# A fixed reserve behind tiles written by GpSimd and by transfers, in the rule that chooses the next instruction of TensorE

## The chip, the cores and the metric

The kernel runs on 1 core of one Trainium2 chip. The metric is the device time of one execution in microseconds; shown is the median of several runs. TensorE (PE) multiplies, VectorE (DVE), ScalarE (ACT) and GpSimd (POOL) do the elementwise work, and SyncE (SP) issues every transfer (DMA). Each engine takes its instructions strictly in the order in which the program lists them for it, and an instruction that needs another engine's result waits on a semaphore, with everything that stands behind it.

## The reference

Four sublayers on a sequence of 2048 rows of 512 numbers: attention with a compressive memory (32 heads of 16, four segments of 512 rows, each causal in itself, and a memory that is carried from segment to segment), a Fourier mixing by two DFT matrices, and both once more.

```python
x = A_x
x = x + _A_ref(_layernorm(x, axis=-1), A_wq, A_wk, A_wv, A_wo, A_beta)
x = x + _B_ref(_layernorm(x, axis=-1), B_dft_seq_re, B_dft_seq_im, B_dft_hid_re, B_dft_hid_im)
x = x + _A_ref(_layernorm(x, axis=-1), A_wq, A_wk, A_wv, A_wo, A_beta)
x = x + _B_ref(_layernorm(x, axis=-1), B_dft_seq_re, B_dft_seq_im, B_dft_hid_re, B_dft_hid_im)

def _A_ref(x, wq, wk, wv, wo, beta):      # q, k, v = x @ w, by heads and segments
    ...
    for s in range(N):
        logits = jnp.einsum("bhqd,bhkd->bhqk", qs, ks) * scale + mask
        p = _softmax(logits, axis=-1)
        a_dot = jnp.einsum("bhqk,bhkd->bhqd", p, vs)
        a_mem = num / den                 # phi(q) @ M  /  phi(q) @ z
        o = g * a_mem + (1.0 - g) * a_dot
        M = M + jnp.einsum("bhld,bhle->bhde", pk, vs)
    ...

def _B_ref(x, dft_seq_re, dft_seq_im, dft_hid_re, dft_hid_im):
    a = jnp.einsum("bsd,ed->bse", x, dft_hid_re)
    b = jnp.einsum("bsd,ed->bse", x, dft_hid_im)
    return jnp.einsum("ts,bse->bte", dft_seq_re, a) - jnp.einsum("ts,bse->bte", dft_seq_im, b)
```

## The kernel before

The work is cut into 32 groups, `i` from 0 to 31: two layers, four segments, four sets of eight heads. Sixteen generators (`streams`) each walk through one kind of work and, as they go, spawn short ones (`tasks`):

- `s_p` projects Q and K of a group, `s_v` projects V. Both multiply the normalized, transposed rows `xt` (tile `g`) with a weight tile. From the second segment on, the weight tile is loaded again from DRAM by `weights.get`, when a slot of its kind (`wt`, `wv`) is free.
- `s_x` computes the scores once for their row maxima: `t_max` on DVE writes them into `mx`, TensorE transposes `mx` by `identf`, and four small transfers write the result into spare rows of `qst`. `s_st` computes the scores a second time, transposed; `t_sel` takes their exponential on ACT into a tile of kind `pt` and masks that tile on GpSimd with `affine_select`; `s_av` multiplies it with `vt`, the values.
- `s_mem` reads and updates the memory `macc`; `s_m` and `t_merge` divide by the denominators through a round trip over DRAM (`den`, `rec`); `s_o` applies `wo`.
- `s_ab` applies the hidden DFT (`wd`), `s_f` the sequence DFT, whose factors `cc` are prepared in `s_c` and kept in DRAM for the second layer. `s_f` and `s_ab` supply the bulk of the wide 128x512 products, and these can stand beside the attention of another segment.

In PSUM all tiles come from one pool of eight banks (named `b`), in SBUF most come from one pool of fifty slots (named `w`); a tile's name carries slot and a running number.

Nothing of the order is written out by hand. While the program is built, the class `Plan` keeps a clock for each engine (`free`), and for each tile the time of its last write (`wr`), its last read (`rd`) and the engine that wrote it last (`by`; `V`, `G`, `A`, `T`, `Y` for DVE, GpSimd, ACT, TensorE, and SP's transfers). Every emitted instruction advances these by a price for its engine, kind and size (`op`). Before an instruction is emitted, a generator yields what it needs (`need`): the engine, the tiles read, the slots wanted. The loop at the end of `body` asks `pl.ready` of all waiting generators for the time at which their need is met, takes the larger of that and the engine's clock, applies a few rules for TensorE (below), and lets the earliest go on; at equal times the first in the list does. So these times decide only which instruction is emitted next. On the chip the semaphores alone hold an instruction back.

TensorE has three modes: `m` for products over the full array, `h` for the scores, which use half of its rows (two at a time), `v` for `s_av`, which uses a quarter of its columns (four at a time). `turn` makes a change of mode dearer in the planner by `SWITCH`, and two blocks in the loop put score work and `s_av` behind other work that is ready.

The price of a transfer in `op` is an issue of 440 ns, 650 ns, its bytes at 360 bytes per ns, and 950 ns behind a load, where the call gives no other estimate: 2768 ns for a weight tile of 256 KB.

Of the kernel before, what the change touches and what calls it, by code (L numbers as in the profile page):

```python
# [31 lines left out]
SLACK = 0  # L32
HOLD, SWITCH = 700.0, 95.0
TWICE, EARLY, BESIDE = 1000.0, 0.0, 1000.0
BATCH = 4
NR = 2


class Plan:
# [80 lines left out]
            ar, b = self.slot[t.tensor.name]  # L120
            self.count[ar["held"].pop(b)] -= 1

    def ready(self, reads, tags):
        r = self.slots_free(tags)
        if r is None:
            return None
        for t in reads:
            n = self.key(t)
            if n in self.fresh:
                return None  # L130
            r = max(r, self.wr.get(n, 0.0))
        return r

    def op(self, eng, name, args, kw):
# [110 lines left out]
def body(ctx: ExitStack, tc: tile.TileContext, x, wq, wk, wv, wo, beta, wd, cs, out):  # L245
    nc = tc.nc
    pl = Plan()
    V, G, A, T, Y = (Eng(e, k, pl) for e, k in zip(
        (nc.vector, nc.gpsimd, nc.scalar, nc.tensor, nc.sync), "VGATY"))
# [59 lines left out]
    def rg(tag, bufs, dt, shape=(128, 512)):  # L309
        return work.tile(list(shape), dt, name=tag, bufs=bufs)  # L310

    def need(eng, *reads, tag=(), mode="m"):
        return eng, reads, (tag,) if isinstance(tag, str) else tag, mode
# [352 lines left out]
    def weights(kind, which):  # L666
        order = [(n, i % NG) for i in range(NG, NGRP) for n in which]
        ready = []

        def get(j, n):  # L670
            if j < NG * len(which):
                yield gate(("W", n, j // len(which)))
                return wnow[n, j // len(which)]
            j -= NG * len(which)
            while len(ready) <= j or len(ready) < len(order) and pl.slots_free((kind,)) is not None:
                n, g = order[len(ready)]
                w = sb(kind, F16, (128, 2, KT, 128))
                Y.dma_start(w, wqkv[g][n])
                ready.append(w)
            return ready[j]  # L680
        return get
# [260 lines left out]
    def width(j):  # L942
        return len(chunks[j][1]) // 2
# [19 lines left out]
    def s_c():  # L963
        k = u = 0
        while u < nunit:
            n = width(units[u][0])
            cam, csc, cgm = (rg(t, 3, F32, (128, BATCH)) for t in ("cam", "csc", "cgm"))
            for i in range(k, k + BATCH):
                yield lambda: len(raws) > i
                yield need("V", raws[i])  # L970
                V.tensor_reduce(cam[:, i - k:i - k + 1], raws[i], axis=AX.X, op=OP.max, apply_absolute_value=True)
            m = BATCH // n
            yield need("T", cam, tag="dft")
# [11 lines left out]
            V.tensor_scalar(fyu[:, u:u + m], gv, f_y, None, op0=OP.mult)  # L985
            for i in range(k, k + BATCH):
                raw, sc = raws[i], csc[:, (i - k) // n:(i - k) // n + 1]
# [11 lines left out]
                done.add(("cd", i))  # L999
            k += BATCH  # L1000
            u += m
# [73 lines left out]
    def settle(s):  # L1075
        while callable(s[0]) and s[0]():
            s[0] = next(s[1], None)
        return s[0] is not None and not callable(s[0])

    while streams or tasks:  # L1080
        best = None
        moved = True
        while moved:
            moved = False
            for s in tasks + streams:
                if callable(s[0]) and s[0]():
                    settle(s)
                    moved = True
        tasks[:] = [s for s in tasks if s[0] is not None]
        streams[:] = [s for s in streams if s[0] is not None]  # L1090
        ready, raw = [], {}
        for s in tasks + streams:
            w = s[0]
            if not callable(w):
                r = pl.ready(w[1], w[2])
                if r is not None:
                    free = pl.turn(w[3]) if w[0] == "T" else min(pl.free[e] for e in w[0])
                    ready.append((max(r, free), s))
                    raw[id(s)] = r
        if pl.mode == "m":  # L1100
            other = min((r for r, s in ready if s[0][0] == "T" and s[0][3] == "m"), default=1e18)
            for j, (r, s) in enumerate(ready):
                if s[0][0] == "T" and s[0][3] == "v" and r >= other:
                    ready[j] = max(r, raw[id(s)] + BESIDE), s
        if pl.mode != "h":
            other = min((r for r, s in ready if s[0][0] == "T" and s[0][3] != "h"), default=1e18)
            for j, (r, s) in enumerate(ready):
                w = s[0]
                if w[2][:2] == ("ss", "ss") and r + EARLY >= other:
                    both = pl.ready(w[1], w[2] + ("ss", "ss"))  # L1110
                    late = raw[id(s)] + TWICE
                    ready[j] = max(r, late if both is None else min(both, late)), s
        if ready:
            first = min(r for r, _ in ready)
            best = next(q for q in ready if q[0] <= first + SLACK)
        if best is None:
            assert not streams and not tasks, "stuck"
            break
        best[1][0] = next(best[1][1], None)
# [45 lines left out]
```

## Time and profile before

| | us |
|---|---|
| median of 3 runs (1844.94 to 1851.16) | 1846.79 |
| the profiled execution's own time | 1845.85 |
| its span, first to last instruction | 1844.1 |
| DVE busy in it | 1086.3 (59%) |
| ACT busy in it | 897.4 (49%) |
| POOL busy in it | 722.6 (39%) |

TensorE's rows stand in the prediction. In all views a name such as `w` stands for every tile of its pool, and every instruction has the line 238, because a helper of the planner issues it; so groups are told apart by names and shapes: `b<-w,g` is the projection of V, `b<-g,w` that of Q or K, `b<-kst,qst` the scores of `s_x` and `b<-qst,kst` those of `s_st`, `b<-w,vt` the work of `s_av`, `b<-w,macc` and `b<-vt,w` reading and updating the memory, `b<-identf,mx` the transposes of the maxima. `w<-w` in a row of a DMA is a transfer between DRAM and a tile of the pool `w`; with TensorE's waits before `b<-w,g` and `b<-g,w` it is a weight tile.

### The profile page before, as it was taken

What the parts mean: (1) busy time and instruction counts of PE and PEld (TensorE: products, weight loads), DVE (VectorE), ACT (ScalarE), POOL (GpSimd) and SP (SyncE); (2) the same over time, 40 slices, a digit from 0 to 9 for tenths busy, and PEclk for the clock granted to TensorE, in tenths of its full rate; (3) what the DMA queues carried; (4) which work ended last, traced back from release to release, by engine and by line L of the source; (5) the groups of instructions that cost most, each with busy time, mean ns of one, the idle gap of its engine ahead of it and who ended that gap; (6) DMA issues with size and microseconds to landing.
All of it is one profiled execution on the core that took longest, in us unless ns stands there. A gap on an engine that the chain in (4) does not pass through costs nothing. (4 is left out here: it accounts for less than half of the span.)

```text
span 1844.1 us, 32657 instructions
## 1 busy us (share of the span) xinstructions
PE 1706.5 (93%) x11045; PEld 744.4 (40%) x11045; DVE 1086.3 (59%) x3406; ACT 897.4 (49%) x1563; POOL 722.6 (39%) x1156
## 2 busy tenths in 40 slices
PE   3878799999999999999899979999999999999999
PEld 2333344443444444344444333433444444434444
DVE  7686774757485786555566655465547565634311
ACT  2546657666647565644447555455444544261000
POOL 3234545546445463553434433433433334052000
PEclk8888999999999999999999988999999999999999
DMA  7345534665466453355774552545345443323233
GB/s 188 103 130 135 146 84 142 183 170 155 122 151 197 127 142 97 110 150 166 225 199 151 168 119 48 142 115 120 106 106 145 120 118 91 90 74 98 92 120 115
DMA packets 240984, 242.44 MB, mean 131 GB/s; under 512 B 129776, under 2 KB 152304, under 8 KB 240816
## 3 DMA queue, kind: packets, MB, share of 16 engines
q1 hardware_dynamic: 240816, 240.35, 47.2%
q8 instruction: 87, 1.43, 0.3%
q14 instruction: 81, 0.66, 0.1%
HBM read 152.96 MB, written 63.70 MB: 117 GB/s over the span
## 5 line engine op out<-in xcount | busy, mean ns | idle before, releaser
L238 PE MATMUL b<-w,w 128*128 128x512 f16 x3072 | 712.3, 380 | 2.6 <-POOL w L238 2.0
L238 PEld LDWEIGHTS <-w 128*128 128x128 f16 x4992 | 462.8, 99 | 623.1 <-issue 130.1
L238 POOL TENSOR_TENSOR w<-w,w 128x512 f16<-128x512 f32 (+1 forms) x314 | 379.4, 1212 | 436.7 <-ACT w L238 271.3
L238 ACT ACTIVATE w<-b,fac 128x512 f32<-128x512 f32 (+1 forms) x728 | 419.4, 655 | 160.9 <-PE b L238 151.7
L238 DVE CUSTOM_DVE_ANT_0 junk<-b,cmask 128x128 bf16<-128x128 f32 (+3 forms) x1024 | 438.7, 486 | 94.8 <-PE b L238 94.0
L238 POOL TENSOR_SCALAR_AFFINE_SELECT w<-w 128x128 f32<-128x128 f32 (+2 forms) x704 | 242.2, 357 | 312.3 <-ACT w L238 306.1
L238 DVE SCALAR_TENSOR_TENSOR y<-b,fyu,y 128x512 f32<-128x512 f32 x200 | 149.4, 747 | 209.0 <-PE b L238 208.4
L238 ACT ACTIVATE w<-b 128x512 f32<-128x512 f32 (+1 forms) x240 | 137.6, 600 | 229.2 <-PE b L238 221.4
L238 ACT ACTIVATE w<-w,csc 128x512 f16<-128x512 f32 (+1 forms) x256 | 181.6, 721 | 57.3 <-DVE csc L238 49.6
L238 PE MATMUL b<-g,w 128*128 128x512 f16 x768 | 194.6, 395 | 13.4 <-issue 9.8
L238 PE MATMUL b<-w,vt 128*32 128x512 f32 (+3 forms) x2048 | 190.0, 451 | 13.2 <-POOL w L238 12.7
L238 PE MATMUL b<-wd,w 128*128 128x512 f16 x768 | 178.1, 380 | 0.0
L238 ACT ACTIVATE w<-w 128x512 f16<-128x512 f32 (+1 forms) x144 | 90.9, 634 | 169.6 <-DVE w L238 135.7
L238 DVE SCALAR_TENSOR_TENSOR w<-b,w 128x512 f16<-128x512 f32 x128 | 87.8, 687 | 134.5 <-ACT w L238 132.1
L238 PE MATMUL b<-kst,qst 62*128 62x128 f16 (+3 forms) x1024 | 127.5, 312 | 11.6 <-ACT w L238 3.5
L238 PE MATMUL b<-qst,kst 64*128 64x512 f16 (+3 forms) x1024 | 120.9, 307 | 15.9 <-ACT w L238 5.4
L238 PE MATMUL b<-w,g 128*128 128x128 f16 x1536 | 102.0, 227 | 19.9 <-DMA w<-w 10.1
L238 PEld LDWEIGHTS <-g 128*128 128x128 f16 x1536 | 93.4, 102 | 35.6 <-issue 17.7
L238 PEld LDWEIGHTS b<-w,vt 128*32 128x32 f32 x2048 | 58.3, 110 | 110.6 <-issue 49.6
L238 PEld LDWEIGHTS <-kst 64*128 64x128 f16 x1024 | 38.1, 94 | 134.3 <-issue 125.8
L238 PE MATMUL b<-wo,w 128*128 128x512 f16 x384 | 91.2, 384 | 0.2 <-DVE w L238 0.2
L238 DVE DVE_READ_ACCUMULATOR2_ANT mx<- 128x1 f32 x1024 | 84.5, 83 | 0.0
(102 smaller groups left out, 889.4 us busy)
## 6 DMA issues: line engine op xcount, KB each, us to landing
w<-in_cs_dram SPq DMA_DIRECT2D x128, 256.0 KB
cc<-w SPq DMA_DIRECT2D x128, 256.0 KB
w<-cc SPq DMA_DIRECT2D x128, 256.0 KB
w<-w SPq DMA_DIRECT2D x96, 256.0 KB
d<-w SPq DMA_DIRECT2D x128, 128.0 KB
w<-rec SPq DMA_DIRECT2D x56, 256.0 KB
w<-in_x_dram SPq DMA_DIRECT2D x32, 256.0 KB
qst<-d SPq DMA_DIRECT2D x64, 128.0 KB
```

The costliest lines, as they stand in the source:

```text
L238: r = f(*args, **kw)
```

## The change

A table of four numbers is added. `ready` now knows the engine that asks, and where TensorE asks, each tile that it would read counts as written later than the planner's time for it: by 500 ns where GpSimd wrote it last, by 1000 ns where a transfer did, by nothing where DVE or ACT did. Other engines ask as before. The times kept in `wr` and in the clocks are not changed, so an instruction that is chosen in spite of the reserve is priced as before.

```diff
+RESERVE = dict(G=500.0, Y=1000.0, V=0.0, A=0.0)
...
-    def ready(self, reads, tags):
+    def ready(self, reads, tags, eng):
...
-            r = max(r, self.wr.get(n, 0.0))
+            r = max(r, self.wr.get(n, 0.0) + (RESERVE.get(self.by.get(n), 0.0) if eng == "T" else 0.0))
...
-                r = pl.ready(w[1], w[2])
+                r = pl.ready(w[1], w[2], w[0])
...
-                    both = pl.ready(w[1], w[2] + ("ss", "ss"))
+                    both = pl.ready(w[1], w[2] + ("ss", "ss"), w[0])
```

The set of products is the same (18016 rows on PE in both programs); their order differs from the first rows on. A running number in a name counts up over all engines as the program is written, so the difference of two numbers tells how much was written between them.

The first place is on PE, the projection of V for the sixteenth group. In the row `b0_9359<-w11_9311,g1_6862` the weight tile `w11_9311` is loaded from DRAM; its load is written where the number 9311 stands. Before:

```order
L238 MATMUL b0_9316<-kst0_102,qst0_104 128x512
L238 MATMUL b7_9320<-kst0_102,qst0_104 128x512
L238 MATMUL b6_9290<-w8_7784,w22_8962 128x512
L238 MATMUL b6_9290<-w17_7825,w22_8962 128x512
L238 MATMUL b2_9344<-wd_141,w27_8460 128x512
L238 MATMUL b0_9359<-w11_9311,g1_6862 128x128
```

and now, where the tile is `w15_9368`:

```order
L239 MATMUL b1_9387<-identf_108,mx_8889 32x128
L239 MATMUL b7_9390<-wd_141,w46_8442 128x512
L239 MATMUL b3_9422<-wd_141,w31_8501 128x512
L239 MATMUL b5_9429<-cam_9396,ones_121 128x4
L239 MATMUL b0_9442<-kst1_103,qst1_105 128x128
L239 MATMUL b4_9457<-kst1_103,qst1_105 128x256
L239 MATMUL b1_9479<-w15_9368,g1_6774 128x128
```

A row stands for all that read the same two tiles. Between the load and the projection stood nine wide products of the DFT (two rows of three on `w22`, one of three on `w27`) and two pairs of scores; now 24 wide ones (twelve on `w46`, twelve on `w31`) and twelve narrow scores stand there, so the distance of the numbers went from 48 to 111.

The second place is on PE too, one of the products of `s_av` in the twentieth group. It reads `pt` tiles, which ACT wrote from the score banks `b4_13856` and `b0_13872` (before) and GpSimd then masked. Before:

```order
L238 MATMUL b1_13692<-w3_13708,vt1_107 32x384
L238 MATMUL b5_13769<-g1_13199,w24_13534 128x512
L238 MATMUL b4_13856<-qst1_105,kst1_103 128x256
L238 MATMUL b0_13872<-qst1_105,kst1_103 128x256
L238 MATMUL b7_13889<-qst1_105,kst1_103 128x128
L238 MATMUL b1_13692<-w48_13862,vt1_107 32x256 x2
```

and now, where the scores are in `b4_13815` and `b6_13826`:

```order
L239 MATMUL b4_13815<-qst1_105,kst1_103 128x256
L239 MATMUL b6_13826<-qst1_105,kst1_103 128x256
L239 MATMUL b2_13751<-g1_13251,w13_13494 128x512
L239 MATMUL b7_13851<-qst1_105,kst1_103 128x128
L239 MATMUL b0_13863<-kst0_102,qst0_104 128x256
L239 MATMUL b5_13874<-g1_13251,w8_13547 128x512
L239 MATMUL b7_13903<-kst0_102,qst0_104 128x384
L239 MATMUL b3_13628<-w34_13821,vt1_107 32x256 x2
```

Before, only eight narrow score products (on `b7_13889` and its partner) stood between the second pair of score banks and the product that reads the masked tile; now 18 wide products of Q and K (nine on `w13`, nine on `w8`) stand there as well.

## The prediction

> **What bounds the kernel now.** I read the page first, for the busy shares, then the waits of PE, the same waits split by stage, and single waits in the order of time.
>
> ```profile
> span 1844.1 us, 32657 instructions
> ...
> PE 1706.5 (93%) x11045; PEld 744.4 (40%) x11045; DVE 1086.3 (59%) x3406; ACT 897.4 (49%) x1563; POOL 722.6 (39%) x1156
> ```
>
> PE is busy for 93% of the span; no other engine reaches 60%. So TensorE is the bound, and the change can only gain where PE stands idle (1844.1 - 1706.5 = 137.6 us) or runs at a lower clock. The idle time before PE's instructions, by what ended it:
>
> ```profile
> PE b L238 <- POOL w L238: 26.9, 26, 5.1
> PE b L238 <- DVE mx L238: 26.3, 22, 3.9
> PE b L238 <- ACT w L238: 17.2, 23, 3.5
> PE b L238 <- DVE amax L238: 16.6, 3, 11.5
> PE b L238 <- DMA w<-w: 11.6, 10, 3.3
> ```
>
> The columns are us in total, times, longest. GpSimd ends 26.9 us; weight tiles that come by transfer end 11.6 us, and with the smaller rows of the split below transfers end 19 us. So some 46 us are all that the two reserves aim at. The rest, DVE and ACT above all, has a reserve of zero. Where these waits stand matters, because a reserve helps only where PE has other work to take:
>
> ```profile
> 0.00:260.00 260.00, 189.47 (x1354) 83.62 (x1355) 196.48 (x684) 129.26 (x230) 97.37 (x171) 0.88 0.52 138
> 260.00:1040.00 780.00, 750.41 (x4853) 333.00 (x4852) 495.97 (x1516) 458.66 (x778) 375.39 (x544) 0.99 0.54 153
> 1040.00:1120.00 80.00, 64.43 (x455) 25.68 (x454) 47.94 (x178) 45.36 (x83) 33.84 (x66) 0.83 0.51 128
> 1120.00:1660.00 540.00, 521.82 (x3552) 220.46 (x3551) 298.24 (x956) 255.05 (x461) 201.78 (x362) 1.00 0.41 107
> 1660.00:1845.00 185.00, 180.41 (x836) 81.61 (x834) 47.70 (x74) 9.09 (x15) 14.26 (x14) 1.00 0.33 106
> ```
>
> The columns are stretch, length, busy time of PE, PEld, DVE, ACT, POOL, then the granted clock, the DMA share and GB/s. In the head (to 260 us) PE is idle for 70.5 us: only the first groups exist there, so other work is scarce. From 260 to 1660 us it is busy 95% of the time, and the reserve can choose among many products; the gain has to come from there. In the last 185 us the sequence DFT runs alone.
>
> ```profile
> PE b L238 <- POOL w L238: 14.3, 12, 5.1
> ...
> PE b L238 <- DMA qst<-mhl: 3.3, 2, 2.5
> ```
>
> ```profile
> PE b L238 <- POOL w L238: 12.6, 14, 2.4
> PE b L238 <- DMA w<-w: 11.6, 10, 3.3
> ...
> PE b L238 <- DMA kst<-d: 2.2, 4, 0.8
> PE b L238 <- DMA g<-w: 1.3, 1, 1.3
> ...
> PE b L238 <- DMA qst<-mhl: 0.6, 1, 0.6
> ```
>
> The first two rows are the waits of the head, the others those after 260 us: 12.6 us behind GpSimd in 14 waits, and 11.6 + 2.2 + 1.3 + 0.6 = 15.7 us behind transfers in 16. With the head's 3.3 us the transfers make 19.0.
>
> **The change, part by part.** Nothing is added to or taken from the work of TensorE; only its order changes, and with it that of what follows on every engine. So the price is a sum of waits. The first three terms can't lie below nothing in themselves, since a reserve only adds work ahead of the reader; what the work taken first costs is the fourth.
>
> *Transfers after 260 us.* Two single rows show what the planner has wrong.
>
> ```profile
> 704.42 0.82 PE L238 MATMUL b<-w,g 128*128 128x128 f16 x6 [3.28 <-DMA w<-w]
> ...
> 1406.11 3.94 DMA w<-w
> ...
> 1530.22 2.75 DMA w<-w
> ...
> 170.65 2.75 PE L238 MATMUL b<-g,w 128*128 128x512 f16 x12
> ```
>
> The first is the longest wait for a weight tile, the next two are steps of the chain that ended last: from issue to landing such a load took 2.75 and 3.94 us. The planner prices it at 2768 ns, so it is right at best and 1.2 us short at worst; a reserve of 1.0 covers most of that. The last row gives the unit in which the order is read: twelve wide products last 2.75 us, 0.23 us each. In the first place of the order nine wide products (2.1 us) and two pairs of scores stood behind the load that PE awaited at 704.42 us; now 24 stand there (5.5 us), more than the slower landing. Counted over the 32 projections of V, the numbers of weight tile and bank are less than 60 apart in 13 before and in 5 now. A reserve of 1.0 us takes at most 1.0 us from each of 16 waits and no more than the 15.7 us that they last; their mean is 0.98 us, and those above 1.0 keep a remainder. Bounds 0 and 15.7 us; I take 11, nearer the upper end, since the order shows the move at the very place of the longest wait.
>
> *GpSimd after 260 us.* Here the reserve is 0.5 us, so it takes at most 14 x 0.5 = 7.0 us of 12.6 by its own size.
>
> ```profile
> 1087.15 0.70 PE L238 MATMUL b<-qst,kst 64*128 64x128 f16 x8 [0.31 <-DVE mx L238]
> 1090.29 1.79 PE L238 MATMUL b<-w,vt 128*32 128x256 f32 x8 [2.43 <-POOL w L238]
> ```
>
> This is the second place of the order: the product ran right behind the scores from which its tiles come and waited 2.43 us for exponential and mask. Now 18 wide products stand between, 18 x 0.23 = 4.1 us, so this wait should go altogether. Over all 704 `pt` tiles, fewer than 16 products of any size stand between the last score product and the first reader in 66 before and 39 now. The share 39/66 leaves 7.4 us of 12.6, which is 5 us less; the single case shows more. Bounds 0 and 12.6; I take 7.
>
> *The head.* 17.6 us of the waits stand there, and PE is idle for 70.5 us because little else is ready. Where no other need is met, the same instruction is chosen as before. By the reserves' own sizes the bounds are 0 and 12 x 0.5 + 2 x 1.0 = 8 us; I take 3, nearer the lower end for that reason.
>
> *What comes back.* What PE takes first is other work with needs of its own, and DVE's reserve is zero. The nearest group is the transposes of the maxima.
>
> ```profile
> L238 PE MATMUL b<-identf,mx 128*32 128x128 f32 x32 | 9.3, 290 | 18.6 <-DVE mx L238 18.6
> ```
>
> Before each of the 32, PE has to have other work while DVE finishes the maxima. At most nine products stand between the last score of `s_x` and the transpose in 13 of them before and in 17 now. Four more at the mean wait of DVE's maxima, 26.3/22 = 1.2 us, are 5 us. Bounds: 5 us less (the four taken the other way), and 26 us more if these waits double. I take 5 us more.
>
> *Everything else.* The order has 960 runs of one mode where it had 977. Seventeen changes fewer are worth between nothing and 17 x 0.3 us (the idle time of 0.31 us in the row at 1087.15, the nearest to a change that costs PE something), and I count them as nothing. The extra delay of 0.5 or 1.0 us on the chains of attention is hidden by the wide products of the DFT up to 1660 us; if that cover were gone at a boundary, one chain of a load, a projection and a masked tile would cost 1.0 + 0.5 us, once. The last stage has no wait of the two kinds and stays at 185 us. SP issues the same transfers, earlier or later with what releases them.
>
> *The sum.* -11 - 7 - 3 + 5 = -16 us against the profiled execution's own time of 1845.85 us: 1829.9. The median of the runs shown, 1846.79, lies 0.9 above the profiled one, so on that scale the time is 1831.
>
> *The clock.* The sum leaves the granted clock as it is. In the stretch from 1040 to 1120 us it was 0.83, and in the last 20 us of it 0.66:
>
> ```profile
> 1100.00:1120.00 20.00, 13.53 (x66) 4.39 (x65) 16.52 (x74) 7.12 (x14) 3.97 (x11) 0.66 0.18 55
> ...
> PE b L238 <- DVE mx L238: 5.6, 4, 3.3
> PE b L238 <- DMA qst<-mhl: 0.6, 1, 0.6
> ```
>
> The last two rows are all of PE's waits in those 20 us; GpSimd ends none of them. The stretch from 1040 us lost (1 - 0.83) x 80 = 13.6 us of full clock, and PE was idle in it for 15.6 us. If fewer idle gaps kept the clock up there, up to 13.6 us more would be gained, though the lowest clock stands beside waits that have no reserve. [...]
>
> **The rivals.**
>
> *Slower: the waits move to DVE.* Score work that PE brings forward gives DVE its maxima in denser bursts, and the transposes queue in order on PE with everything behind them. For it speaks that DVE is the second busiest engine (59%), that its waits already equal those of GpSimd, and the 17 against 13 above; against it that the counts moved little. If all 32 transposes waited 2.0 us, between the mean of 1.2 and the longest of 3.9, that would be 64 - 26 = 38 us more. With the 21 us gained above, the time is 1846.8 - 21 + 38 = 1864. It is slower than before by 0.3% (5.5 us, about what a measurement of this kernel can tell from no change) from 26.5 us of new waits on, that is, when the maxima cost 53 us in place of 26.3.
>
> *No change: the gap moves on by one instruction.*
>
> ```profile
> POOL w L238 <- ACT w L238: 577.4, 477, 26.9
> ACT w L238 <- PE b L238: 373.2, 197, 39.6
> ```
>
> POOL is late because ACT is: the masks wait for the exponentials, and these for PE. If the work taken first leads to a tile of ACT, which has no reserve, PE waits there instead (17.2 us now). The order speaks against it for transfers, where no such chain follows. If half the gain after 260 us is lost in this way, 9 us of 18, the time is 1831 + 9 = 1840; with the head's 3 us gone too, 1843.
>
> *More than forecast: the clock.* If the stretch around 1100 us runs at full clock, 1831 - 13.6 = 1817. The head, at 0.88, would give more, but its idle time stays.
>
> *The change does nothing.* The order rules it out: both places have moved.
>
> **How the numbers follow.** The forecast, 1831 with 1823 to 1841 around it, has 0.50. The clock (to 1817) has 0.13, no change (1841 to 1852) 0.19, slower 0.18. Faster by more than 0.3% is the first two, 0.63; within 0.3% 0.19; slower 0.18. The range runs from 1815, just below the clock's case, to 1856, which takes in no change and the lesser part of slower; some 0.05 is left below and 0.12 above.
>
> **What would show it.** In the changed kernel's waits of PE, `DMA w<-w` should fall from 11.6 to under 4 us and `POOL w` from 26.9 to about 17, almost all of it after 260 us; `DVE mx` should be 26 to 35. PE's busy time should stay within 3 us of 1706.5 and the last stage at 185 us. The forecast is wrong if `DVE mx` and `ACT w` together grow by more than 20 us, or if a PE busy time that has moved shows that the clock, and not the waits, set the result.

## The result and the profile after

The changed kernel takes 1815.8 us (median of 4 runs, 1814.1 to 1820.3) against 1846.9 us before: ratio 0.983 (95% interval 0.980 to 0.985), 31 us or 1.7% faster. The forecast was 1831 us, so its direction held and its size was half of what came; the time lies inside the range, at its lower end, next to the rival in which the clock adds to the gain (1817 us). The profiled execution is the fastest of the four, with a mean granted clock of 0.974; the other three show 0.969 to 0.973.

First the page of the changed kernel, span and busy shares.

```profile
span 1812.4 us, 32639 instructions
...
PE 1697.2 (94%) x11045; PEld 739.2 (41%) x11045; DVE 1086.6 (60%) x3408; ACT 898.1 (50%) x1563; POOL 718.5 (40%) x1154
```

Of the 31.7 us by which the span fell, PE's idle time gave 22.4 (137.6 to 1812.4 - 1697.2 = 115.2). The other 9.3 us are busy time of PE (1706.5 to 1697.2), though its work is the same. Next PE's waits, longest first: us in total, times, longest.

```profile
PE b L239 <- DVE mx L239: 26.1, 38, 3.7
PE b L239 <- ACT w L239: 17.7, 37, 3.5
PE b L239 <- DVE amax L239: 16.4, 2, 11.5
PE b L239 <- POOL w L239: 13.1, 12, 3.5
PE b L239 <- DMA g<-w: 5.9, 2, 3.8
PE b L239 <- DMA w<-w: 5.8, 6, 1.7
PE b L239 <- issue: 5.6, 2, 5.2
```

GpSimd fell from 26.9 to 13.1 us, weight tiles from 11.6 to 5.8, the maxima of DVE stayed where they were. But transfers of all kinds together only fell from 19.3 to 16.6 us: the waits for transposed rows (`g<-w`) were 1.3 us and are 5.9. Then the stages, in the columns of the prediction; they are cut at the same times as before, so in the faster kernel each holds a little more of the work.

```profile
0.00:260.00 260.00, 197.70 (x1376) 85.07 (x1377) 197.37 (x695) 135.44 (x239) 99.69 (x181) 0.88 0.51 138
260.00:1040.00 780.00, 754.45 (x4939) 331.73 (x4937) 512.45 (x1550) 465.99 (x792) 381.58 (x555) 0.99 0.54 156
1040.00:1120.00 80.00, 64.44 (x467) 27.41 (x467) 43.24 (x163) 43.73 (x79) 32.54 (x60) 0.89 0.44 113
1120.00:1660.00 540.00, 532.00 (x3584) 227.79 (x3579) 299.42 (x953) 246.91 (x445) 198.86 (x352) 1.00 0.42 111
```

PE's idle time fell by 8.2 us in the head (62.3 left of 70.5), by 4.0 up to 1040 us, and by 10.2 from 1120 to 1660. From 1040 to 1120 us it is as idle as before, at a clock of 0.89 in place of 0.83. In the head the waits of the two kinds are now these, the columns as above:

```profile
PE b L239 <- DVE mx L239: 16.5, 19, 3.7
...
PE b L239 <- POOL w L239: 4.7, 7, 2.0
...
PE b L239 <- DMA qst<-mhl: 0.8, 1, 0.8
PE b L239 <- DMA kst<-d: 0.6, 2, 0.3
```

Last, the two places whose order was shown, and one more, from PE's instructions in the order of time: start, duration, instruction, and in brackets the idle time before it.

```profile
696.40 1.50 PE L239 MATMUL b<-w,g 128*128 128x128 f16 x24
...
1053.52 1.13 PE L239 MATMUL b<-w,macc 64*128 64x512 f32 x4 [3.48 <-POOL w L239]
...
1074.28 1.51 PE L239 MATMUL b<-w,vt 128*32 128x256 f32 x32
```

The first row is the projection of V that had waited 3.28 us for its weight tile, the third the product of `s_av` that had waited 2.43 us for its mask: neither waits any more. The second row shows that a new long wait behind GpSimd has come up between them, at the read of the memory.

### The profile page after: what moved, and what is told of

The parts are those of the page before. It is cut to its first block, busy times and chain, and to the rows that moved or that the text cites. A ratio compares the mean times of both kernels' runs of the same rounds, so it can differ in the third digit from the quotient of the medians.

```text
span 1812.4 us, 32639 instructions
## 1 busy us (share of the span) xinstructions
PE 1697.2 (94%) x11045; PEld 739.2 (41%) x11045; DVE 1086.6 (60%) x3408; ACT 898.1 (50%) x1563; POOL 718.5 (40%) x1154
## 5 line engine op out<-in xcount | busy, mean ns | idle before, releaser
L239 ACT ACTIVATE w<-b 128x512 f16<-128x512 f32 (+1 forms) x240 | 137.5, 598 | 229.6 <-PE b L239 221.3
L239 PE MATMUL b<-g,w 128*128 128x512 f16 x768 | 195.4, 399 | 11.6 <-DMA g<-w 5.9
L239 PE MATMUL b<-w,vt 128*32 128x512 f32 (+3 forms) x2048 | 186.3, 458 | 4.5 <-POOL w L239 4.0
L239 PEld LDWEIGHTS <-g 128*128 128x128 f16 x1536 | 90.1, 100 | 26.5 <-issue 19.3
```

The costliest lines, as they stand in the source:

```text
L239: r = f(*args, **kw)
```

## The experiments

Theory A: a reserve removes waits of its own kind, because work stands where PE had waited, and nothing else matters much. Theory B: every new order is a new draw, that is, an accident of many small differences, and the change drew a good one. All ratios are against the kernel before on the same chip in the same session, since its median moved between 1840.7 and 1849.6 us from session to session. Times are medians of all executions; waits and busy times come from the one profiled execution of each kernel.

### One reserve at a time, halved, doubled

```diff
-RESERVE = dict(G=500.0, Y=1000.0, V=0.0, A=0.0)
+RESERVE = dict(G=500.0, Y=0.0, V=0.0, A=0.0)       # e1_g_only
+RESERVE = dict(G=0.0, Y=1000.0, V=0.0, A=0.0)      # e2_y_only
+RESERVE = dict(G=250.0, Y=500.0, V=0.0, A=0.0)     # e3_half
+RESERVE = dict(G=1000.0, Y=2000.0, V=0.0, A=0.0)   # e4_double
```

GpSimd's alone:

> Reserve of 0.5 us behind GpSimd kept, that behind transfers set to 0. Theory A (each reserve removes the waits of its own kind, and the clock's loss falls with the idle time): PE's waits behind POOL near 13 us as in the change, those behind transfers near 19 us as before; 1820 to 1828 us, since GpSimd gave 13.8 of the 22 us of idle time that went. Theory B (any new order of this size is a new draw, and the kinds do not matter): the waits of both kinds anywhere between 13 and 30 us, the time anywhere from 1810 to 1850.

Measured: 1825.3 us, ratio 0.989 (0.985 to 0.992); waits behind POOL 13.5 us, behind transfers 19.3, as A expected.

That of the transfers alone:

> Reserve of 1.0 us behind transfers kept, that behind GpSimd set to 0. Theory A: waits behind POOL near 27 us as before, those behind transfers 13 to 17 us; 1836 to 1844 us. Theory B: the time anywhere from 1810 to 1850, POOL's waits not tied to the reserve.

Measured: 1841.9 us, ratio 0.998 (0.996 to 1.000); transfers 13.1 us, as A has it, but POOL 18.0 in place of 27: a kind of wait that had no reserve fell by 9 us. The time hardly shows these 15 us: PE's idle time fell by 11.4 us in all, but its busy time rose by 7.5, at a lower clock (0.962 in the profiled execution).

Both halved:

> Both reserves halved (0.25 and 0.5 us). Theory A: about half the gain, 1828 to 1836 us, POOL's waits 17 to 22 us. Theory B: no order in the sizes; the time may lie below the change's 1815 or above 1840.

Measured: 1836.9 us, ratio 0.995 (0.993 to 0.997); POOL 15.4 us, transfers 27.4. The time is near A's range (0.9 us above it), but POOL's waits are below the range that A gave, and the transfers' are above those of before.

Both doubled:

> Both reserves doubled (1.0 and 2.0 us). Theory A: POOL's waits 6 to 11 us, those behind transfers under 12 us, 1806 to 1815 us as long as PE has other work; if the work taken first is what waits next, DVE's and ACT's waits grow and it is 1815 to 1825. Theory B: anywhere from 1810 to 1850.

Measured: 1811.3 us, ratio 0.981 (0.978 to 0.984); POOL 10.1 us, transfers 6.4, as A expected. So the times follow the size of the reserve from half to single (the doubled one cannot be told from the single), but single kinds of waits do not always.

### The control, and a reserve for all

```diff
-RESERVE = dict(G=500.0, Y=1000.0, V=0.0, A=0.0)
+RESERVE = dict(G=0.0, Y=0.0, V=500.0, A=500.0)       # e5_va_only
+RESERVE = dict(G=500.0, Y=1000.0, V=500.0, A=500.0)  # e6_all
```

> The control: reserves behind GpSimd and transfers 0, 0.5 us behind DVE and ACT in their place. The order is redrawn as much as by the change, but not aimed at the 46 us of waits. Theory A: POOL's waits 22 to 30 us and transfers' 16 to 22 us as before; ACT's and DVE's waits fall by up to 10 us; 1836 to 1848 us. Theory B: a gain as likely as with the change, POOL's waits anywhere from 13 to 30 us.

Measured: 1837.1 us, ratio 0.995 (0.993 to 0.996). From PE's waits in this kernel:

```profile
PE b L239 <- DVE mx L239: 21.9, 29, 4.5
...
PE b L239 <- POOL w L239: 15.7, 21, 3.2
PE b L239 <- DMA qst<-mhl: 14.9, 10, 5.6
PE b L239 <- DMA w<-w: 10.5, 11, 1.9
```

A's time holds, and so does what it says of the kinds that have a reserve here: all waits behind ACT fell from 19.2 to 10.2 us, those behind DVE from 55.4 to 49.7. What it says of the other kinds does not: POOL fell to 15.7 us with no reserve behind it, and transfers doubled to 41 us. Waits move between kinds with every order, so one kind in one profile does not show what a reserve is worth.

> The change, and 0.5 us behind DVE and ACT too. Theory A: the waits of the four kinds all at or below those of the change, 1805 to 1815 us; if a reserve for all kinds is only a delay for all (the ranks among the ready stay as they were), the gain of the change shrinks to 1820 to 1835. Theory B: 1805 to 1845.

Measured: 1831.5 us, ratio 0.992 (0.989 to 0.995); POOL 14.6 us, transfers 25.2, the maxima 23.2. That is half of the change's gain, as the second possibility of A says. But the run does not show that the added reserves cost anything: the nudged orders below, with the two reserves alone, stand at 0.993 to 0.995, so the loss can as well be the new order's.

### Only in the head, only behind it

```diff
-(RESERVE.get(self.by.get(n), 0.0) if eng == "T" else 0.0)
+(RESERVE.get(self.by.get(n), 0.0) if eng == "T" and self.free["T"] < 260e3 else 0.0)    # e7_head
+(RESERVE.get(self.by.get(n), 0.0) if eng == "T" and self.free["T"] >= 260e3 else 0.0)   # e8_tail
```

> The reserves hold only while the planner's clock of PE is below 260 us, and are 0 behind that. If the gain of the head (8.2 us less idle time there) is the reserve's own doing: 1834 to 1840 us, with the head's waits as in the change (POOL near 5 us) and those behind it near those of before. Theory B: the head as in the change, since its order is the same; behind it anything, 1815 to 1845.

Measured: 1852.4 us, ratio 1.003 (1.001 to 1.005). The head's waits behind POOL are 4.8 us, near the 4.7 of the change, whose order the head repeats, and still the kernel is slower than before: over the whole span the maxima cost 32.9 us in place of 26.3, and PE is busy for 1713.3 us in place of 1706.5.

> The reserves are 0 while the planner's clock of PE is below 260 us and hold behind that. Theory A: the head's waits as before (POOL near 14 us, idle near 70 us), those behind it as in the change or below; 1820 to 1828 us. With the run that has them only in the head, the two gains add up to the change's 31 us to within 6 us. Theory B: they don't add up.

Measured: 1840.8 us, ratio 0.995 (0.993 to 0.998), with 13.3 us behind POOL in the head, as before. A falls here as far as it says that nothing else matters much: +0.3% and -0.5% are not the change's -1.7%. The parts do not add up; the order behind 260 us is another one in each of the three kernels.

### The same order nudged, without and with the reserves

This asks how much of a gain is the reserve's and how much the draw's. A price of the planner that means nothing on the chip is moved by one or two ns; each nudge is run without reserves, with those of the change, and two of them with doubled ones.

```diff
-HOLD, SWITCH = 700.0, 95.0
+HOLD, SWITCH = 700.0, 96.0                            # n1
-    LAT = dict(T=197.0, V=150.0, A=165.0, G=100.0, Y=0.0)
+    LAT = dict(T=197.0, V=150.0, A=167.0, G=100.0, Y=0.0)   # n3
+    LAT = dict(T=197.0, V=152.0, A=165.0, G=100.0, Y=0.0)   # n4
+    LAT = dict(T=199.0, V=150.0, A=165.0, G=100.0, Y=0.0)   # n5
```

> A neutral redraw: no reserve, the planner's price of a change of mode 96 in place of 95 ns, which means nothing on the chip but gives another order from the twentieth part of the program on. If a new order alone moves the time by little: within 5 us of before (1841 to 1852). If the order of before was an unlucky draw: 10 to 25 us faster, with POOL's waits near 16 to 20 us.

> The same nudge with the two reserves of the change. If the reserves carry the gain: 20 to 35 us below its partner without them, POOL's waits 10 to 15 us, transfers' 12 to 18 us. If the change's order was a lucky draw: less than 12 us below its partner.

> A second neutral redraw: no reserve, the planner's latency behind ACT 167 in place of 165 ns. As for the first: within 5 us of before if the draw matters little; 10 to 25 us faster if before was unlucky.

> The second nudge with the two reserves. 20 to 35 us below its partner if the reserves carry the gain; less than 12 us if the change's order was lucky.

> A third neutral redraw: no reserve, the planner's latency behind DVE 152 in place of 150 ns. If the draw is worth a few us only, as in the two before: 1835 to 1852 us. If reserves are what matters, POOL's and the transfers' waits together stay above 35 us.

> The third nudge with the two reserves. If the reserves give about 1% on the mean and the change's order was lucky: 8 to 25 us below its partner, 1820 to 1835 us. If the reserves carry the change's whole gain: 28 us or more below, near 1815.

> A fourth neutral redraw: no reserve, the planner's latency behind PE 199 in place of 197 ns. 1835 to 1852 us; POOL's and the transfers' waits together above 35 us.

> The fourth nudge with the two reserves. 8 to 25 us below its partner, 1820 to 1835 us, if the reserves give about 1% on the mean; near 1815 if they carry the whole gain.

> The first nudge (mode change 96 in place of 95 ns) with both reserves doubled. If the size of the reserve decides (transfers' waits fall as 19, 17, 6 us for 0, 1.0 and 2.0 us): transfers' waits 4 to 10 us, POOL's 7 to 12 us, 1808 to 1822 us, below its partner with the single reserves. If the draw decides: within 8 us of that partner or above it.

> The second nudge (latency behind ACT 167 in place of 165 ns) with both reserves doubled. Transfers' waits 4 to 10 us, POOL's 7 to 12 us and 1808 to 1822 us if the size of the reserve decides; within 8 us of its partner with the single reserves, or above it, if the draw does.

Measured, as ratios to the kernel before (with the 95% interval):

| order | no reserve | 0.5 and 1.0 us | 1.0 and 2.0 us |
|---|---|---|---|
| that of the change | 1 | 0.983 (0.980 to 0.985) | 0.981 (0.978 to 0.984) |
| n1 | 1.004 (1.002 to 1.006) | 0.993 (0.991 to 0.996) | 0.981 (0.979 to 0.984) |
| n3 | 0.997 (0.995 to 0.999) | 0.995 (0.992 to 0.997) | 0.982 (0.979 to 0.985) |
| n4 | 1.000 (0.998 to 1.002) | 0.995 (0.993 to 0.998) | not run |
| n5 | 0.998 (0.996 to 1.001) | 0.993 (0.989 to 0.996) | not run |

And from the profiles, the mean over the orders of each column, in us (sums of PE's waits by what ended them; in brackets the lowest and the highest order):

| | no reserve (5) | 0.5 and 1.0 us (5) | 1.0 and 2.0 us (3) |
|---|---|---|---|
| behind POOL and transfers together | 46.2 (44.0 to 48.4) | 30.1 (26.5 to 33.1) | 18.8 (16.5 to 23.4) |
| behind DVE's maxima | 28.5 (26.3 to 33.0) | 32.4 (26.1 to 41.6) | 24.9 (23.9 to 25.5) |
| PE idle in all | 137.2 (133.6 to 142.1) | 123.6 (115.2 to 131.1) | 113.2 (109.6 to 116.4) |
| PE busy | 1704.5 (1702.7 to 1706.5) | 1703.7 (1697.2 to 1708.5) | 1701.4 (1700.2 to 1702.9) |

The first row is the clearest: the sum of the two kinds hardly depends on the order (44 to 48 us in five orders), though its split does (POOL 9.9 to 30.9 us), and it falls with the reserve without overlap. So the reserves do remove the waits they are aimed at, as a sum, in every order. The two kinds take part in it differently: the waits behind POOL are 22.3 us on the mean without reserves, 10.8 with the single and 11.1 with the doubled ones; those behind transfers are 23.8, 19.4 and 7.7, and with the single reserves they rose in two orders (n1 and n5). So the single reserves work on GpSimd above all, and what the doubled ones add is the transfers. What the whole gives is another matter. These are the largest waits of PE in n3 without reserves,

```profile
PE b L239 <- DVE mx L239: 33.0, 37, 5.5
PE b L239 <- POOL w L239: 20.3, 23, 3.3
PE b L239 <- DVE amax L239: 17.3, 4, 11.5
PE b L239 <- DMA qst<-mhl: 12.2, 4, 5.3
```

with the single ones,

```profile
PE b L239 <- DVE mx L239: 41.6, 54, 3.7
PE b L239 <- DVE amax L239: 16.4, 2, 11.5
PE b L239 <- POOL w L239: 11.4, 16, 2.0
```

and with the doubled ones.

```profile
PE b L239 <- DVE mx L239: 23.9, 39, 4.1
PE b L239 <- ACT w L239: 20.0, 26, 3.4
PE b L239 <- DVE amax L239: 16.6, 3, 11.5
PE b L239 <- POOL w L239: 9.2, 10, 3.1
```

With the single reserves 8.6 us of what was gained behind POOL and transfers (48.4 to 26.5) came back in front of the transposes of the maxima. With the doubled ones nothing came back there.

Over the five orders the single reserves give 1.73, 1.08, 0.25, 0.45 and 0.59% against their partners, 0.8% or 15 us on the mean. The change's order is 1% better than the mean of the four others with the same reserves (0.994). The doubled reserves give 1.8 to 1.9% below the kernel before in three orders out of three (1.9, 2.3 and 1.5% against their partners): the version to take, though in the change's own order the two cannot be told apart (0.983 and 0.981, with overlapping intervals).

## Why the prediction was half right

*What bounds the kernel.* Right: the gain came out of PE's idle time and its clock, and the busy times of DVE, ACT and POOL changed by 4.1 us at most.

*Transfers after 260 us, -11.* The step was right about the place (the wait of 3.28 us is gone) and about weight tiles, which fell by 5.8 us over the span. As a sum it failed: 15.9 us (the 15.7 of the prediction and a row of 0.2 us that it left out) became 15.1, because 4.6 us more are spent before transposed rows and 2.0 us before a tile of the division. On the mean of the five orders these waits fell by 2.0 us (19.0 to 17.0), not by 11. Doubling the reserve brought all transfers to 6 to 9 us, so 1.0 us was too small for them (the transfers' reserve was not doubled alone); the landing of 3.94 us against the planner's 2.77 is 1.17 us short already.

*GpSimd after 260 us, -7.* 12.6 became 8.5, so -4.1; the new wait of 3.48 us at 1053 us is more than the 2.9 us that are missing. On the mean of the five orders it was -6.1, near the forecast.

*The head, -3.* Mis-sized: GpSimd gave 9.6 us there and transfers 1.9, of which the maxima took back 3.1. The argument that nothing else is ready in the head was wrong, and so was the bound of 8 us: a reserve can take more from a wait than its own size, because the work that it lets in may be much longer (24 wide products in place of nine, in the first place of the order). On the mean of the five orders GpSimd gave 5.5 us in the head (10.6 to 5.1) and transfers 2.4, and the maxima took back 3.0; the rest is this order's own.

*What comes back, +5.* In this order nothing came back (26.3 to 26.1 us). Over the five orders it was +3.9, so the term was right on the mean and the change's order escaped it; that of n3 paid 8.6.

*The sum.* The four terms add to -16; measured, POOL, transfers and maxima gave -13.8 - 2.7 - 0.2 = -16.7. The sum of the waits that it spoke of was right by luck: the mistakes of the terms cancelled.

*The clock, 0.* This is the step that failed: "The sum leaves the granted clock as it is." PE's busy time fell by 9.3 us with the same products. The mean clock rose from 0.969 to 0.974, and the time lost to it, one minus the clock times the span, fell from 57 to 47 us, which is the same 10 us within rounding. The rival that named the clock, "If the stretch around 1100 us runs at full clock", saw the place of about half of this, but a third of its 13.6 us came: from 1040 to 1120 us the clock gave (0.89 - 0.83) x 80 = 4.8 us.

No run shows that a new order leaves the clock as it is; the profiled executions of the 20 programs show means of 0.962 to 0.974, and in the kernel before the clock fell within single waits. Here is the clock (third number from the end) in the kernel before, around and behind the two waits that the prediction picked out, of 3.28 and of 2.43 us, and the first work behind the former:

```profile
703.50:710.50 7.00, 6.08 (x52) 5.16 (x52) 1.91 (x5) 0.08 (x1) 0.00 (x0) 0.51 0.48 139
1089.00:1096.00 7.00, 5.71 (x48) 2.41 (x49) 2.51 (x12) 2.77 (x6) 4.60 (x8) 0.52 0.87 189
...
704.42 2.74 PE L238 MATMUL b<-w,g 128*128 128x128 f16 x24 [3.28 <-DMA w<-w]
```

and in the changed kernel around the three rows shown with the result:

```profile
690.00:720.00 30.00, 30.00 (x204) 12.82 (x205) 20.10 (x71) 18.54 (x35) 12.84 (x24) 1.00 0.39 121
1046.00:1061.00 15.00, 9.65 (x72) 3.99 (x72) 4.23 (x7) 11.40 (x21) 6.91 (x12) 1.00 0.68 178
1070.00:1080.00 10.00, 10.00 (x121) 5.85 (x119) 7.04 (x25) 6.72 (x12) 5.45 (x9) 1.00 0.39 108
```

The clock was halved for some 7 us from within each of the two waits on, which is 3.4 us of full clock each, all but some 0.5 us of it behind the wait (0.9 and 1.0 us of the low clock lie within it); 24 products of V took 2.74 us there and take 1.50 now. With the waits both losses are gone, and others have come elsewhere, such as one of 3.4 us from 887.5 us on. Not every wait is followed by one: that of 3.48 us at 1053 us leaves the clock at 1.00. Which waits are followed so was not found, and no run changes the clock alone.

Nor do the reserves raise the clock on the mean. It differs between executions of one kernel: 0.966 to 0.977 in the 106 of the kernel before that were run beside the experiments (mean 0.970, 56 us lost), 0.969 to 0.974 in the four of the change (mean 0.972, 51 us lost). So of the 9.3 us in the profiled pair about 5 are left on the mean, which four executions hardly tell from nothing. The four nudged orders have mean clocks of 0.970 without the reserves and of 0.966 to 0.970 with them.

*Everything else, 0.* This failed too, by less: the remaining 5.7 us of idle time fell in kinds of waits that no term had, most of it in the row "issue" (10.0 to 5.6 us, one wait of 4.5 us fewer). What ends that wait the profile does not show.

*Its own signs.* Weight tiles were to fall under 4 us and are at 5.8; POOL was to fall to about 17 us almost only after 260 us, and fell to 13.1, most of it in the head; PE's busy time left its 3 us, the sign that the clock had a part.

So, as far as five orders tell, the gain beyond the forecast is the draw: a forecast of 0.9% met a mean effect of 0.8%, and an order that lies 1% below the mean of its kind. The prediction took the order's own accidents for a few us and had no term for them. In the four redraws without reserves they were -0.3 to +0.4%, in those with the single reserves 0.2% around their mean; the change, which was run in one session only, lies far outside of that.

*The rivals.* Slower, by more waits behind DVE: it did not happen in the change, but its mechanism is real: in n3 it took back 8.6 of 21.9 us, and where the reserves held only in the head the maxima rose by 6.6 us. No change, by the gap moving on to ACT: not seen, the waits behind `ACT w` are 17.7 us against 17.2.

## What to carry to other kernels

Where a planner's clock decides an order, the waits of one kind in one profile are an accident; nudge a price that means nothing a few times, with and without the change, and compare the pairs. Size a reserve by the planner's worst shortfall, not its mean one: the transfers, late by up to 1.17 us in the rows shown, gave little with 1.0 us and most of their waits with 2.0. Against their partners the single reserves gave 0.3 to 1.7% depending on the order, the doubled ones 1.5 to 2.3%. Look at the clock behind a wait before pricing the wait at its own length: in the kernel before, from within the waits of 3.28 and of 2.43 us on, it was at about half for some 7 us, 3.4 us of full clock each. A gain in one order can be half luck, and the next edit may lose it.

## What the runs showed of the hardware

PE's busy time less the time lost to the clock, with the clock as the profile gives it to three places, is 1649 us before and 1650 after, and 1637 to 1652 us in the 18 other programs, whose products are the same: so the spans differ by idle time and clock, with up to 15 us left over. The clock's loss did not go with the idle time: 56 us at 109.6 us of idle time (both reserves doubled), 57 us at 137.6 (before), 70 us at 126.2 (the transfers' reserve alone). In the profiled executions of the kernel before and of the change, read in windows of 0.5 us, each stretch of low clock loses 1.7 us of full clock or a multiple of it (to 6.8 us), leaving aside the last half us of the kernel before. In the kernel before, the clock fell from 1.00 to 0.50 at 1089.3 us, 1.4 us into the wait of 2.43 us, and at 703.6 us within that of 3.28 us; the wait of 3.48 us in the changed kernel left it at 1.00.
